# Dealing the keys of a K or V half tile by sixteenths of the head instead of by halves

## The chip, the cores and the metric

The kernel runs on one core of one Trainium2 chip. The metric is the device time of one execution in microseconds (us). Runs of one kernel agree within about 0.3% in most executions; the three runs of the kernel before gave 311.65, 312.02 and 314.75 us, with a median of 312.02 us.

## The reference: two layers of attention over a cache and a gated GLU, one token each

Four sequences (B = 4) decode one token through two layers with the same weights and the same cache. Each layer adds grouped-query attention and then a gated linear unit to the residual x.

```python
def _A_ref(x, k_cache, v_cache, wq, wo):          # x: [4, 1, 512]
    q = (x @ wq).reshape(B, Sq, Hq, Dh)...        # Hq = 32 heads of Dh = 128
    k = jnp.repeat(k_cache, rep, axis=1)          # k_cache: [4, 8, 4096, 128] bf16, rep = 4
    v = jnp.repeat(v_cache, rep, axis=1)
    scores = jnp.einsum("bhqd,bhkd->bhqk", q, k) * (Dh ** -0.5)
    p = _softmax(scores, axis=-1)
    o = jnp.einsum("bhqk,bhkd->bhqd", p, v)
    return o... @ wo

def _B_ref(x, w_gate, w_up, w_down):              # F = 1792
    h = _sigmoid(x @ w_gate) * (x @ w_up)
    return h @ w_down

x = x + _A_ref(_layernorm(x), ...)
x = x + _B_ref(_layernorm(x), ...)
x = x + _A_ref(_layernorm(x), ...)                # the same cache and weights again
x = x + _B_ref(_layernorm(x), ...)
```

A head of the cache has 4096 keys of 128 bf16 numbers, 256 bytes a key and 1 MB a head. Softmax and the sum over the keys don't depend on the order of the keys, as long as K and V are put in the same order.

## The kernel before: units, half tiles and a ring of 23 slots

**Units.** The attention is cut into 16 units (b, hg, l): sequence, group of four cache heads (NS = 4 heads s of the group), layer. `UNITS` gives their order. The heads of hg = 1 stay in SBUF between the layers, so a unit (b, 1, 1) loads nothing; every other unit loads its four heads of K and of V. `unit_scores`, `unit_probs` and `unit_values` write the work of a unit.

**Half tiles.** A head of K or V is loaded in two half tiles q = 0 and 1 of 2048 keys: `load_kv` (lines 508 to 516) issues one DMA of 512 KB from the queue of SyncE (SP) at line 514. Its destination is a slot of `ring`, 128 partitions by `TH * DH` = 2048 bf16 numbers, so 4 KB in each partition: 16 keys. Its source (line 513) is a run of 512 KB of the head, the front half of the head for q = 0 and the back half for q = 1. Partition p gets keys 16p to 16p + 15 of that half.

**Loads.** There are 192 such DMAs (96 of K and 96 of V), 100.7 MB of the 114.6 MB that the kernel reads. The rest are the weights: `wq` in two loads (line 519, 2 MB each), `wo` in four of 1 MB, and `wg`, `wu`, `wd` of 1.75 MB each. `LOADS` fixes the order of all loads by hand; a word such as K0000 stands for two half tiles (two heads s of one q). K comes with q outermost, V with the pair of heads outermost.

**Order of the work.** `_Plan.schedule` places every operation in a simulated time with costs written beside it (a K or V load has `size=0.524, cost=0.5`), chooses a ring slot for each load (the slot that comes free first of 23), and adds matmuls into a scratch bank (line 1105) where TensorE would idle. `emit` then writes the instructions of each engine with waits on semaphores. A load waits on SP for the last user of its slot.

**Use.** A K half tile is transposed in place by VectorE (line 723, 32 by 32 blocks of pairs of bf16), four matmuls of each half tile read it into the scores (line 731), VectorE takes the maximum (754 to 761), ScalarE the exponential (line 768), and the probabilities are transposed and spread (774, 779, 789). The values matmuls (line 815) read V slots as they lie. Nothing in these lines names a key by its place in the head: the key in partition p, place t of slot q of K meets the key in the same place of V.

Of the kernel before, what the change touches and what calls it, by code (L numbers as in the profile page):

```python
# [350 lines left out]
def bass_interleave_layers__gqa_block_cached__glu_gated_glu__decode_kernel(nc, A_x, A_k, A_v, A_wq, A_wo, B_x, B_wg, B_wu, B_wd, out):  # L351
# [5 lines left out]
    P = 128  # L357
# [4 lines left out]
    NS = 4  # L362
# [4 lines left out]
    TH = T // 2  # L367
# [127 lines left out]
    def tile(kind, b, hg, l, s, q):  # L495
        if l == 1 and hg == 1 and (s, q) in kept[kind]:
            l = 0
        key = (kind, b, hg, l, s, q)
        if key not in tiles:
            tiles[key] = _Tile(key)  # L500
        return tiles[key]

    def fresh(kind, hg, l, s, q):
        return not (l == 1 and hg == 1 and (s, q) in kept[kind])
# [3 lines left out]
    def load_kv(kind, u, s, q):  # L508
        b, hg, l = u
        if not fresh(kind, hg, l, s, q):  # L510
            return
        t = tile(kind, b, hg, l, s, q)
        src = (A_k if kind == "k" else A_v)[b, hg * NS + s, q * TH * P:(q + 1) * TH * P].rearrange("(p t) d -> p (t d)", p=P)
        S.put("sp", lambda e: e.dma_start(ring[t.slot], src), dma="ring", load=t, size=0.524, cost=0.5)  # L514
        sent[0] += 0.524 / DMA_RATE
        place[kind, u, s, q] = sent[0]
# [33 lines left out]
    for word in LOADS.split():  # L550
        if word[:2] == "wq":
            load_wq(int(word[2]))
        elif word[:2] == "wo":
            load_wo(int(word[2]))
        elif word[0] == "w":
            load_glu(word)
        else:
            for piece in pieces(word[0], word[1:]):
                load_kv(*piece)
# [586 lines left out]
```

## Time and profile before

| what | value |
|---|---|
| median of 3 runs | 312.02 us (311.65 to 314.75) |
| the profiled execution | 312.2 us, span 310.5 us |
| bytes read from HBM | 114.56 MB, 369 GB/s over the span |
| packets of SP's queue (q1) | 34832, 94.6% of 16 DMA engines' span |
| VectorE (DVE) busy | 168.1 us (54%) |
| TensorE (PE) busy | 213.2 us (69%), 50.5 us of it fillers of line 1105 |
| ScalarE (ACT) busy | 60.8 us (20%) |
| K and V loads, issue to landing | medians 9.7 and 10.2 us |

The span is the time from the first to the last instruction of the profiled execution; 1.7 us of that execution lie outside it. The page cuts the span into 40 slices of 7.8 us; the row GB/s has what the DMA engines moved in each. A packet is what one of the 16 DMA engines moves as one piece; SP's queue has 128 packets of 4 KB for a half tile and 16 packets of 4 bytes that raise the semaphore.

### The profile page before, as it was taken

The numbers are of one execution on the slowest core, as the hardware profiler recorded it, in microseconds if no ns is written. First come the engines' busy times: TensorE is split into PE (matmuls) and PEld (weight loads), VectorE is DVE, ScalarE is ACT, GpSimd is POOL, SyncE is SP. The second block draws the span as 40 slices with busy tenths as digits, with TensorE's granted clock in tenths as the row PEclk, the third lists the DMA queues.
The fourth block names the chain that finished last, engine by engine and source line by source line (L and its number), as shares of the span: only waits on it lengthen the run. The fifth ranks groups of instructions, "written<-read, shape, count | busy, mean of one in ns | idle before, by whom it ended". The sixth has DMA issues, their size and how long they took to land.

```text
span 310.5 us, 7729 instructions
## 1 busy us (share of the span) xinstructions
PE 213.2 (69%) x3395; PEld 114.2 (37%) x3395; DVE 168.1 (54%) x314; ACT 60.8 (20%) x151; POOL 12.6 (4%) x44
## 2 busy tenths in 40 slices
PE   1344446577838976776996866885974757788694
PEld 1213114433425632243553422462431424534243
DVE  3675542483001699596217863736996952475112
ACT  0202002002101312021323120131330213231301
POOL 8000000000000000000000000000000000000001
PEclk9999999959995998599978877997897999979859
DMA  7999999999999999999999999799999999999900
GB/s 265 411 408 410 409 388 348 395 410 409 404 397 411 402 409 407 407 411 395 380 413 385 409 410 406 283 340 408 331 414 410 408 401 373 394 352 411 391 9 4
DMA packets 34931, 115.09 MB, mean 371 GB/s; under 512 B 3280, under 2 KB 7376, under 8 KB 34896
## 3 DMA queue, kind: packets, MB, share of 16 engines
q1 hardware_dynamic: 34832, 114.57, 94.6%
q8 instruction: 27, 0.44, 0.6%
q14 instruction: 8, 0.07, 0.1%
q10 hardware_dynamic: 64, 0.01, 0.0%
HBM read 114.56 MB, written 0.00 MB: 369 GB/s over the span
## 4 chain that ended last, share of the span: by engine, by line
DMA 57%; PE 25%; DVE 8%; SPq 4%; issue 3%; ACT 3%; POOL 1%; DVEq 0%; ACTq 0%
DMA ring<-in_A_k_cache_dram 20%; DMA ring<-in_A_v_cache_dram 17%; DMA wd<-in_B_w_down_dram 7%; PE S_ps L731 7%; DMA wq<-in_A_wq_dram 6%; DMA wo<-in_A_wo_dram 5%; PE O_ps L815 5%; DVE ring L723 4%; SPq L514 3%; PE M_ps L850 2%; PE Q_ps L651 2%; PE G_ps L954 1%; PE PT_ps L1105 1%; SPq L519 1%; PE PT_ps L779 1%
## 5 line engine op out<-in xcount | busy, mean ns | idle before, releaser
L723 DVE STREAM_TRANSPOSE ring<-ring 128x1024 int32<-128x1024 int32 x96 | 116.1, 1227 | 33.4 <-DMA ring<-in_A_k_cache_dram 32.6
L731 PE MATMUL S_ps<-ring,qz 128*32 128x512 bf16 x512 | 48.4, 505 | 32.7 <-DVE ring L723 26.0
L815 PE MATMUL O_ps<-ring,pt_sb 128*16 128x512 bf16 x512 | 45.4, 442 | 20.5 <-DMA ring<-in_A_v_cache_dram 17.5
L1105 PE MATMUL PT_ps<-even 128*128 128x256 bf16 x305 | 50.5, 305 | 8.9 <-ACT pp L932 4.3
L1105 PEld LDWEIGHTS PT_ps<-even 128*128 128x128 bf16 x305 | 29.1, 109 | 27.5 <-issue 9.8
L827 ACT ACTIVATE b<-O_ps 128x512 bf16<-128x512 f32 x32 | 19.1, 596 | 85.3 <-PE O_ps L815 81.8
L731 PEld LDWEIGHTS S_ps<-ring,qz 128*32 128x32 bf16 x512 | 13.9, 113 | 55.5 <-DVE ring L723 31.5
L768 ACT ACTIVATE pp<-S_ps,tr 128x512 bf16<-128x512 f32 x16 | 13.2, 828 | 50.4 <-DVE tr L761 48.5
L754 DVE TENSOR_REDUCE stat<-S_ps 128x1 f32<-128x512 f32 x16 | 11.1, 692 | 21.9 <-PE S_ps L731 21.8
L815 PEld LDWEIGHTS O_ps<-ring,pt_sb 128*16 128x16 bf16 x512 | 9.7, 89 | 32.8 <-issue 13.1
L850 PE MATMUL M_ps<-oT,wo 128*128 128x32 bf16 x512 | 15.8, 178 | 2.0 <-DMA wo<-in_A_wo_dram 1.6
L839 DVE TENSOR_TENSOR oT<-M_ps,rl 128x8 bf16<-128x8 f32 x32 | 4.9, 152 | 22.7 <-PE M_ps L832 22.7
L850 PEld LDWEIGHTS M_ps<-oT,wo 128*128 128x128 bf16 x512 | 14.1, 97 | 7.3 <-DVE oT L839 2.9
L902 POOL TENSOR_TENSOR stat<-stat 128x1 f32<-128x1 f32 x8 | 4.4, 545 | 256.2 <-ACT stat L898 256.2
L789 ACT ACTIVATE pt_sb<-PT_ps 128x512 bf16<-128x512 f32 x16 | 9.6, 597 | 17.6 <-PE PT_ps L779 17.6
L832 PE MATMUL M_ps<-sel_o,b 128*128 128x32 bf16 x128 | 8.7, 183 | 4.7 <-ACT b L827 4.6
L832 PEld LDWEIGHTS M_ps<-sel_o,b 128*128 128x128 bf16 x128 | 5.8, 101 | 16.1 <-ACT b L827 12.3
L937 DVE SCALAR_TENSOR_TENSOR b<-pp,U_ps 128x448 bf16<-128x448 f32 (+2 forms) x6 | 3.2, 538 | 14.5 <-ACT pp L932 12.9
L695 ACT ACTIVATE maskrs<-mask,stat 128x16 f32<-128x16 f32 x16 | 4.5, 304 | 28.5 <-DVE qz L700 26.5
L793 PE MATMUL M_ps<-sel_h,stat 128*128 128x16 f32 x32 | 6.7, 286 | 4.4 <-ACT pp L768 4.1
L774 DVE STREAM_TRANSPOSE pp<-pp 128x256 int32<-128x256 int32 x16 | 6.8, 426 | 5.2 <-ACT pp L768 5.2
L700 DVE TENSOR_TENSOR qz<-Q_ps,maskrs 128x256 bf16<-128x256 f32 x16 | 6.3, 394 | 6.0 <-PE Q_ps L690 6.0
(112 smaller groups left out, 162.6 us busy)
## 6 DMA issues: line engine op xcount, KB each, us to landing
ring<-in_A_k_cache_dram SPq DMA_DIRECT2D x96, 512.0 KB, 9.7
ring<-in_A_v_cache_dram SPq DMA_DIRECT2D x96, 512.0 KB, 10.2
wq<-in_A_wq_dram SPq DMA_DIRECT2D x2, 2048.0 KB, 13.8
wo<-in_A_wo_dram SPq DMA_DIRECT2D x4, 1024.0 KB, 14.7
wg<-in_B_w_gate_dram SPq DMA_DIRECT2D x1, 1792.0 KB, 16.1
wu<-in_B_w_up_dram SPq DMA_DIRECT2D x1, 1792.0 KB, 20.2
wd<-in_B_w_down_dram SPq DMA_DIRECT2D x1, 1792.0 KB, 22.7
xin<-in_A_x_dram ACTq DMA_DIRECT2D x1, 4.0 KB, 3.4
```

The costliest lines, as they stand in the source:

```text
L514: S.put("sp", lambda e: e.dma_start(ring[t.slot], src), dma="ring", load=t, size=0.524, cost=0.5)
L723: "dve", lambda e, t=t: e.transpose(ring[t.slot].bitcast(dt.int32), ring[t.slot].bitcast(dt.int32)),
L731: fns.append(lambda e, s=s, t=t, nn=nn, q=q: e.matmul(S_ps[qi][32 * s:32 * s + 32, :], lhsT=window(qi, s * NQ + nn, q), rhs=ring[t.slot].r ...
L754: dve(lambda e: e.tensor_reduce(ml[at], bank, AX.X, ALU.max, negate=True), keys(f"S{qi}", ss), keys("ml", ss), 0.7)
L768: lambda e: e.activation(p_sb[at].rearrange("p (t j r) -> p t r j", j=32, r=2), bank.rearrange("p (t r j) -> p t r j", r=2, j=32), ACTF.Ex ...
L774: dve(lambda e: e.transpose(pd[at].bitcast(dt.int32), p_sb[at].bitcast(dt.int32)), [own("P")], [own("P") + "d"], 0.4)
L789: "act", lambda e: e.activation(pt_sb[qi][:, cols], PT_ps[:, cols], ACTF.Copy),
L815: fns.append(lambda e, m=m, at=at, v=v, c=c, q=q: e.matmul(O_ps[m:m + 16, :], lhsT=pt[:, at:at + 16], rhs=ring[v.slot][:, c * 512:(c + 1) ...
L827: "act", lambda e: e.activation(b1[:], O_ps[:], ACTF.Copy),
L832: fns.append(lambda e, tt=tt: e.matmul(M_ps[:, 0:WIDE], lhsT=b1[:, tt * P:(tt + 1) * P], rhs=sel_o[:, tt, :].unsqueeze(1).broadcast_to([P, ...
L850: fns.append(lambda e, k=k, n=n, h0=h0: e.matmul(M_ps[:, k * WIDE:(k + 1) * WIDE], lhsT=wo[:, h0 + n, k * P:(k + 1) * P], rhs=oT[:, b, h0 ...
L1105: S.filler(lambda e: e.matmul(PT_ps[:, 0:256], lhsT=ident, rhs=flat_even[:, 0:256], start=True, stop=True), "PT")
```

## The change: the half of each sixteenth

```diff
@@ load_kv
         t = tile(kind, b, hg, l, s, q)
-        src = (A_k if kind == "k" else A_v)[b, hg * NS + s, q * TH * P:(q + 1) * TH * P].rearrange("(p t) d -> p (t d)", p=P)
+
+        src = (A_k if kind == "k" else A_v)[b, hg * NS + s].rearrange("(e h j t) d -> h e j (t d)", e=16, h=2, j=8)[q]
         S.put("sp", lambda e: e.dma_start(ring[t.slot], src), dma="ring", load=t, size=0.524, cost=0.5)
```

The head is cut into 16 stretches e of 256 keys (64 KB). Each stretch has a front half and a back half h of 128 keys (32 KB), and each half has 8 groups j of t = 16 keys (4 KB). Half tile q takes half h = q of every stretch, so its source is now a pattern of 16 by 8 by 2048 numbers: 16 pieces of 32 KB whose starts lie 64 KB apart. Partition 8e + j gets group j of piece e. K and V change alike. Sizes, the order of the loads, the ring, the plan's costs and every other instruction stay.

## The prediction

> **What bounds the kernel now.** I read the page first, from its slices and queues to the chain, then the windows, then the ring's own view, then SP's waits. The page:
>
> ```profile
> span 310.5 us, 7729 instructions
> ...
> DMA  7999999999999999999999999799999999999900
> GB/s 265 411 408 410 409 388 348 395 410 409 404 397 411 402 409 407 407 411 395 380 413 385 409 410 406 283 340 408 331 414 410 408 401 373 394 352 411 391 9 4
> ...
> q1 hardware_dynamic: 34832, 114.57, 94.6%
> ...
> DMA 57%; PE 25%; DVE 8%; SPq 4%; issue 3%; ACT 3%; POOL 1%; DVEq 0%; ACTq 0%
> ```
>
> The DMA engines are busy in nearly every slice until the loads end, and slice after slice stands at 407 to 411 GB/s. The chain that ended last is 57% DMA. So the stream of loads bounds the kernel, and the rate of that stream is what any change of a load is worth. The windows (columns: stretch, its length, busy time of PE, PEld, DVE, ACT and POOL with instruction counts, granted clock, DMA share, GB/s) show what sets the rate:
>
> ```profile
> 13.00:25.00 12.00, 4.01 (x36) 1.09 (x36) 8.81 (x12) 1.41 (x4) 0.00 (x0) 1.00 1.02 408
> 48.00:52.00 4.00, 2.39 (x59) 2.00 (x58) 1.03 (x4) 1.35 (x3) 0.00 (x0) 1.00 1.10 348
> 112.00:128.00 16.00, 10.25 (x125) 4.92 (x121) 15.46 (x20) 3.05 (x7) 0.00 (x0) 0.79 1.03 409
> 187.00:197.00 10.00, 7.92 (x118) 4.13 (x119) 5.06 (x9) 0.60 (x1) 0.00 (x0) 0.83 1.03 408
> 197.00:206.00 9.00, 6.71 (x122) 3.37 (x120) 4.84 (x12) 3.33 (x9) 0.54 (x1) 1.00 0.73 259
> 206.00:220.00 14.00, 10.65 (x214) 6.06 (x209) 8.18 (x17) 2.21 (x9) 0.55 (x1) 0.77 0.95 370
> 270.00:283.00 13.00, 11.21 (x157) 4.38 (x157) 8.76 (x16) 4.24 (x11) 0.00 (x0) 0.87 0.95 364
> 283.00:296.00 13.00, 9.91 (x188) 5.49 (x188) 3.81 (x13) 2.71 (x6) 0.00 (x0) 0.84 0.93 371
> ```
>
> With K and V in flight (112 to 128, 187 to 197) the engines are full (share 1.03) and move 409 GB/s. A packet of 4096 bytes then takes 16 x 4096 / 409 GB/s = 160 ns, and a half tile, 8 packets on each of 16 engines, 1.28 us. At 48 to 52 us `wo` comes in packets of 1 KB and the rate is 348 GB/s, 47.1 ns a packet. So 3 KB more cost 113.1 ns, 37.7 ns a KB, and 9.4 ns of each packet don't depend on its size. The last four rows have the engines partly idle or slow: against 409 GB/s they lose 9 x (1 - 259/409) = 3.3, then 1.3, 1.4 and 1.2 us, in all 7 us.
>
> ```profile
> L514 SPq DMA_DIRECT2D ring<-in_A_k_cache_dram x96: 327/433/4366, 1.3 to 275.0; - x96
> L514 SPq DMA_DIRECT2D ring<-in_A_v_cache_dram x96: 327/433/12672, 12.3 to 282.1; - x96
> ...
> DMA to landing us min/median/max: 3.7/10.0/23.4
> ```
>
> SP needs 433 ns (median) for an issue, a third of the 1.28 us that the load then takes, and a load lands 10.0 us after its issue: about eight half tiles stand in the queue. SP's own waits are for slots:
>
> ```profile
> SPq L514 <- PE O_ps L815: 26.0, 12, 9.0
> ...
> SPq L514 <- PE S_ps L731: 10.5, 8, 4.6
> ```
>
> These waits are for readers of old tiles and mostly lie under the eight tiles still queued.
>
> **The change part by part.** Removed and added instructions: none. There are still 192 DMAs of 512 KB on the same queue in the same order; the plan sees the same `size` and `cost`, so every engine's program and the slots stay. Keys move between the halves in K and V alike, so the sums see the same pairs.
>
> *Addresses in HBM.* A tile's source is 16 pieces of 32 KB with gaps of 32 KB instead of one run. `wq` is the nearest row: its packets are 4 KB rows 8 KB apart, so eight neighbouring partitions start 64 KB from the next eight. It is in flight up to 25 us, mixed with K and V, at 408 GB/s, the rate of K and V alone. Price 0. Bound: 408 against 409 is 0.25% of 192 x 1.28 = 246 us, 0.6 us.
>
> *SP.* The issue has a source of three dimensions now. `wq` had three too, and its first issue takes 0.41 us in the timeline of SP. Price 0, hidden under the eight queued tiles. If an issue took twice 433 ns it would still be under 1.28 us; only where the queue has run dry (around 197 us, and at the head) would 0.43 us show, three or four times: up to 2 us.
>
> *Which engine writes which partition.* This is the open part. [...] Now the source counts 16 first, and each of those stretches fills partitions 8e to 8e + 7. An engine that takes one stretch writes eight neighbouring partitions, and must. The trace doesn't show which partitions an engine wrote before, nor what two engines cost each other when they write through one way into SBUF. The lower bound is nothing: a packet stays at 160 ns, and 1.28 us a tile. The upper bound is that, in step, two engines always share what one had: 320 ns a packet, 2.56 us a tile, 246 us more. [...] If the two run in step, but data in flight lets one packet of each four escape, the factor is 1.75; if they run exactly out of step it is 1.0. I take the middle, 1.375, because nothing in the plan puts the engines in or out of step. Cost 0.375 x 246 = 92 us.
>
> [...]
>
> *What a slower stream gives back.* The 7 us in which the stream lagged behind readers or slots go, since compute then has more time for each tile. DVE's 168 us and PE's 213 us hide under the loads. The weights (13.9 MB) and the tail of 14 us after the last landing stay.
>
> **Sum.** 310.5 + 92 - 7 = 395.5 us of span, and 1.7 us outside it: 397 us. The profiled execution's 312.2 us stand 0.2 us over the median of the runs, so no shift is needed. With the bounds of the factor alone the case reaches from 312 to 551 us; what I count as this case is a factor of 1.15 to 1.85, 342 to 514 us.
>
> **Rivals.**
>
> *Nothing happens: 312 us.* The queue may deal the rows as before, or the meetings may be hidden by data in flight, or the change doesn't do what it says at the engines. For it: `wq` shows that addresses alone cost nothing, and SP and the plan don't change. Against it: the engines have no slack (share 1.03), so any extra wait of a packet shows in full.
>
> *The reads become longer: faster, 305 us.* The 32 KB of an engine are one straight piece, and could be read as one packet instead of eight. Seven of eight fixed costs of 9.4 ns go, 8.2 ns of 160 for each 4 KB: 5.1% of 246 us, 12.6 us. Only 57% of the chain is DMA, so some 7 us arrive: 305 us; all of it would be 299. For it: the 348 and 409 GB/s of the two packet sizes. Against it: the pattern still names 8 groups of 2048 numbers, and before, where the whole 512 KB was straight, packets were 4 KB.
>
> *The meetings stay rare: 324 us.* Engines that start in step part quickly, each meeting pushing one behind the other until they alternate. Then only the beginnings pay: a factor of 1.05 is 12 us. For it: the stretches that lose rate make the engines start anew only a few times. It ends slower, like the forecast, but its profile would show about 390 GB/s.
>
> **How the numbers follow.** Forecast (partners meet) 0.50; rare meetings 0.14; nothing 0.16; longer reads 0.20. A difference of under 1% can't be told from no change here. Of "nothing", 0.13 lies within 1%, and of the rest half falls on each side; of "longer reads", 0.01 falls within 1%. Faster 0.015 + 0.19, about 0.21; same 0.14; slower 0.50 + 0.14 + 0.015, about 0.65. The range leaves out 0.1 below, where longer reads arrive nearly in full, and 0.1 above, where partners run nearly in step: 302 to 490 us. It is wide because one unknown factor between 1 and 2 stands on 246 us of a stream that bounds the kernel.
>
> **What the profile after would show.** Instructions stay at 7729. If I am right, the slices of K and V stand well under 409 GB/s with the DMA share still near 1, at about 300 GB/s; the slices with `wo`, `wg`, `wu` and `wd` alone keep 348 to 400; a load lands later than 10.0 us after issue; VectorE's waits for K (32.6 us) and the values' waits for V (17.5 us) grow; the chain is more than 57% DMA; SP's waits for slots shrink. If packets of q1 fall from 34832 to some 13000, the reads became longer. If GB/s stays at 409 with the same packets, partners don't meet, and I was wrong in the term of the dealing. A lower rate in the slices of the weights alone would mean that something other than the dealing slowed the engines.

## The result: 447.7 us against 312.0 us, and the profile after

The median of four runs is 447.74 us (442.38 to 453.05), that of before 312.0 us. The ratio is 1.419, with a 95% interval of 1.405 to 1.432. It is taken over undisturbed runs alone, so it is a little smaller than the quotient of the two medians. The profiled execution took 445.58 us, with a span of 443.9 us.

From the page of the profile after: the span, the DMA share and GB/s of the 40 slices (now 11.1 us each), SP's queue, and the engines' shares of the chain.

```profile
span 443.9 us, 7729 instructions
...
DMA  8999999999999999999999999899999999999950
GB/s 260 241 307 247 247 245 346 251 259 260 376 287 255 254 256 261 259 261 270 284 298 285 296 296 299 244 239 244 252 262 266 266 277 265 259 255 249 248 140 3
...
q1 hardware_dynamic: 34832, 114.57, 98.0%
...
DMA 67%; PE 14%; SPq 12%; DVE 4%; issue 2%; ACT 1%; POOL 0%; DVEq 0%
```

The same 34832 packets keep the engines busier than before (98.0% of the span, up from 94.6%), and move 239 to 299 GB/s where K and V are loaded, down from 410. Only slices with much weight traffic stand out, at 307, 346 and 376 GB/s. The packets' own time shows where the difference went:

- Time that packets of SP's queue took, per engine: 0.946 x 310.5 = 293.7 us before, 0.980 x 443.9 = 435.0 us after, 141.3 us more.
- The span grew by 443.9 - 310.5 = 133.4 us. The sum of packet times is not the time in which the engines are busy: packets of a full engine overlap, and a window with full engines stands at a share of 1.03. So the rest of the span, 16.8 us before and 8.9 us after, is not idle time; the stretch after the last landing alone is 14.0 us before and 14.3 us after.

If all of the 141.3 us belongs to the 246 us of K and V, a packet of 4 KB takes 1.57 times as long, 252 ns. The windows after agree (columns as in the prediction; the first two have weights in flight, the third K and V, the last nothing):

```profile
73.00:78.00 5.00, 3.98 (x51) 3.21 (x52) 0.16 (x1) 0.00 (x0) 0.00 (x0) 1.00 1.13 352
117.00:122.00 5.00, 4.13 (x39) 2.59 (x37) 0.41 (x3) 0.73 (x4) 0.55 (x1) 0.90 1.03 400
290.00:405.00 115.00, 72.02 (x1013) 35.79 (x1013) 50.70 (x88) 19.18 (x51) 1.62 (x3) 0.67 1.03 258
429.60:443.90 14.30, 10.12 (x154) 5.34 (x154) 3.23 (x17) 1.82 (x5) 1.01 (x1) 0.74 0.01 3
```

`wo` keeps its rate (352 GB/s, 348 before), and so do the weights of the GLU (400 GB/s; 399 at 80 to 92 us before). Their lines of the program did not change. Only K and V are slower, at 258 GB/s or 16 x 4096 / 258 = 254 ns a packet.

From the ring's own view of the profile after (each line: operation, count, duration in ns as min/median/max), and from the waits:

```profile
L515 SPq DMA_DIRECT2D ring<-in_A_k_cache_dram x96: 536/599/6136, 1.3 to 394.1; - x96
L515 SPq DMA_DIRECT2D ring<-in_A_v_cache_dram x96: 536/598/17772, 15.4 to 405.1; - x96
...
DMA to landing us min/median/max: 5.0/16.4/30.2
```

```profile
DVE ring L724 <- DMA ring<-in_A_k_cache_dram: 112.5, 78, 8.1
PE O_ps L816 <- DMA ring<-in_A_v_cache_dram: 82.3, 33, 11.4
```

An issue on SP takes 599 ns instead of 433, a load lands 16.4 us after its issue instead of 10.0, and VectorE's waits for K and the values' waits for V have grown from 32.6 and 17.5 us to these. Nothing else on the engines explains 133 us: VectorE is busy for 172.3 us, 4 more than before. TensorE is busy for 246.4 us instead of 213.2, at a granted clock of 0.741 instead of 0.899, but its share of the chain fell from 25% to 14%. Why the clock fell is not shown. SP's share of the chain rose from 4% to 12%. Most of that lies in the first 47 us, where many of its issues last 1.8 to 2.1 us while the engines are full (share 1.03). This fits an SP that is held up by a full queue; no run separates it.

### The profile page after: what moved, and what is told of

It reads as the page before. It is cut to its first block, busy times and chain, and to the rows that moved or that the text cites. A ratio compares the mean times of both kernels' runs of the same rounds, so it can differ in the third digit from the quotient of the medians.

```text
span 443.9 us, 7729 instructions
## 1 busy us (share of the span) xinstructions
PE 246.4 (56%) x3395; PEld 124.4 (28%) x3395; DVE 172.3 (39%) x314; ACT 60.5 (14%) x151; POOL 12.5 (3%) x44
## 3 DMA queue, kind: packets, MB, share of 16 engines
q1 hardware_dynamic: 34832, 114.57, 98.0%
## 4 chain that ended last, share of the span: by engine, by line
DMA 67%; PE 14%; SPq 12%; DVE 4%; issue 2%; ACT 1%; POOL 0%; DVEq 0%
DMA ring<-in_A_v_cache_dram 31%; DMA ring<-in_A_k_cache_dram 29%; SPq L515 11%; DMA wo<-in_A_wo_dram 6%; PE O_ps L816 4%; PE S_ps L732 4%; DVE ring L724 2%; PE PT_ps L1106 1%; PE G_ps L913 1%; PE M_ps L851 1%; PE U_ps L913 1%; SPq L520 1%; PE G_ps L955 1%; DVE stat L755 0%; PE M_ps L833 0%
## 5 line engine op out<-in xcount | busy, mean ns | idle before, releaser
L724 DVE STREAM_TRANSPOSE ring<-ring 128x1024 int32<-128x1024 int32 x96 | 118.7, 1239 | 112.8 <-DMA ring<-in_A_k_cache_dram 112.5
L816 PE MATMUL O_ps<-ring,pt_sb 128*16 128x512 bf16 x512 | 55.0, 521 | 86.0 <-DMA ring<-in_A_v_cache_dram 82.3
L732 PE MATMUL S_ps<-ring,qz 128*32 128x512 bf16 x512 | 51.9, 534 | 61.3 <-DVE ring L724 49.0
L1106 PE MATMUL PT_ps<-even 128*128 128x256 bf16 x305 | 60.3, 347 | 9.8 <-ACT pp L933 5.3
L1106 PEld LDWEIGHTS PT_ps<-even 128*128 128x128 bf16 x305 | 32.2, 119 | 33.2 <-issue 11.6
L828 ACT ACTIVATE b<-O_ps 128x512 bf16<-128x512 f32 x32 | 19.1, 597 | 143.5 <-PE O_ps L816 141.3
L851 PE MATMUL M_ps<-oT,wo 128*128 128x32 bf16 x512 | 16.7, 185 | 3.9 <-DVE oT L840 2.2
L780 PE MATMUL PT_ps<-pp,even 128*32 128x128 bf16 x256 | 9.2, 288 | 3.0 <-DVE oT L840 2.0
L794 PE MATMUL M_ps<-sel_h,stat 128*128 128x16 f32 x32 | 8.5, 346 | 2.3 <-ACT pp L769 2.0
```

Of the source, the lines that this page charges most:

```text
L724: "dve", lambda e, t=t: e.transpose(ring[t.slot].bitcast(dt.int32), ring[t.slot].bitcast(dt.int32)),
L732: fns.append(lambda e, s=s, t=t, nn=nn, q=q: e.matmul(S_ps[qi][32 * s:32 * s + 32, :], lhsT=window(qi, s * NQ + nn, q), rhs=ring[t.slot].r ...
L780: fns.append(lambda e, s=s, a=a: e.matmul(PT_ps[32 * a:32 * a + 32, s * P:(s + 1) * P], lhsT=ident[at, 32 * s:32 * s + 32], rhs=spread[:, ...
L816: fns.append(lambda e, m=m, at=at, v=v, c=c, q=q: e.matmul(O_ps[m:m + 16, :], lhsT=pt[:, at:at + 16], rhs=ring[v.slot][:, c * 512:(c + 1) ...
L828: "act", lambda e: e.activation(b1[:], O_ps[:], ACTF.Copy),
L851: fns.append(lambda e, k=k, n=n, h0=h0: e.matmul(M_ps[:, k * WIDE:(k + 1) * WIDE], lhsT=wo[:, h0 + n, k * P:(k + 1) * P], rhs=oT[:, b, h0 ...
```

## The experiments

Theory 1 is that of the forecast: the dealing of eight neighbouring partitions to one engine makes engines meet on the way into SBUF. Theory 2 blames the gaps between the pieces in HBM. Theory 3 blames the source of three dimensions, which takes longer to issue or to expand, wherever its rows land. In what follows, "dealt by 128" and "dealt by 16" say what the source counts first.

### Addresses alone (e1)

```diff
-        src = ...[b, hg * NS + s, q * TH * P:(q + 1) * TH * P].rearrange("(p t) d -> p (t d)", p=P)
+        src = ...[b, hg * NS + s].rearrange("(p h t) d -> h p (t d)", p=P, h=2)[q]
```

> Addresses alone: a half tile is the front or back 4 KB of each 8 KB of the head, so it is spread over the whole 1 MB as in the change, but source and destination both count 128 rows. Theory 1 (the dealing of eight neighbouring partitions to one engine makes engines meet on the SBUF side): about 312 us, 409 GB/s in the slices of K and V, 160 ns a packet. Theory 2 (the gaps between the pieces in HBM slow the reads): well over 400 us, slices near 260 GB/s.

328.37 us against 314.59 us of before on the same chip: ratio 1.045 (1.040 to 1.050). Both theories missed the size. Spreading a half tile over 1 MB in pieces of 4 KB does cost something, 14 us, but a tenth of what the change cost. From the page, the slices:

```profile
GB/s 272 390 410 390 354 393 350 399 412 407 401 401 374 352 412 410 408 335 347 383 353 340 407 411 409 277 354 389 329 410 388 367 366 372 300 282 366 401 48 4
```

Some stretches run at 407 to 412 GB/s like before, others at 277 to 393; before has about half as many slices below 395. Theory 2 can't be the main cause. What slows these stretches is taken up in e5.

### Dealing alone (e2)

```diff
-        src = ...[b, hg * NS + s, q * TH * P:(q + 1) * TH * P].rearrange("(p t) d -> p (t d)", p=P)
+        src = ...[b, hg * NS + s, q * TH * P:(q + 1) * TH * P].rearrange("(j e t) d -> e j (t d)", e=16, j=8)
```

> [...] Theory 1: 440 to 455 us, slices of K and V near 255 GB/s. Theory 2: about 312 us. Theory 3 (a source of three dimensions is slower to issue or to expand into descriptors, wherever the rows land): 440 to 455 us as well; the next kernel tells 1 from 3.

The median is 456.06 us (446.15 to 467.16). The profiled execution took 452.26 us with a span of 450.5 us, against 445.58 and 443.9 us for the change. The tile is the same run of 512 KB as before, counted 16 first (4 KB apart) and then 8 (64 KB apart), and all of the loss is there. From its page:

```profile
GB/s 265 249 307 249 250 256 330 248 248 249 393 262 254 255 260 262 262 270 280 278 286 299 304 316 315 195 232 232 233 235 236 235 241 241 244 252 258 268 165 3
...
q1 hardware_dynamic: 34832, 114.57, 98.0%
```

The slices have the form of the change's own, at the same share of 98.0%. Theory 2 has fallen as the main cause; theories 1 and 3 stand.

### Loads alone, and where the rows land (e3)

```python
...
# stage e; stage f is the same with partitions (0, 64)
for i in range(36):
    load(e, slot(i, (32, 96)), heads[i].rearrange("(e h j t) d -> h e j (t d)", e=16, h=4, j=4)[0])
...
```

> Loads alone: all of the computation is left out and zeros are written. Stages follow each other, each of 24 half tiles of 512 KB without a wait between them: a the source of before, b that of the change, c the spread one dealt by 128, d the run dealt by 16; then 36 loads of 256 KB with a source of 16 pieces of 16 KB, e into partitions 32 to 95 and f into partitions 0 to 63; then a and b again. Theory 1: a and c near 409 GB/s, b and d 220 to 300. [...] Theory 2: a, d near 409, b, c, e, f slower. Theory 3: a, c near 409, b, d, e, f slower, and e as f.

Windows inside the stages a, b, c, d, e and f, in this order (stretch, its length, busy time of POOL, granted clock, DMA share, GB/s):

```profile
8.00:28.00 20.00, 0.00 (x0) 1.00 1.02 411
38.00:84.00 46.00, 0.00 (x0) 1.00 1.03 246
94.00:112.00 18.00, 0.00 (x0) 1.00 1.03 412
125.00:172.00 47.00, 0.00 (x0) 1.00 1.03 237
188.00:200.00 12.00, 0.00 (x0) 1.00 1.03 411
210.00:250.00 40.00, 0.00 (x0) 1.00 1.03 200
```

Stages e and f have the same sources, the same dimensions, the same number of issues on SP and the same packets. Only the partitions differ: 32 to 95 run at 411 GB/s, 0 to 63 at 200. That ends theory 3: a source of three dimensions runs at 411 GB/s, the rate of stage a, in partitions 32 to 95. Shown is that the place of the rows in SBUF alone can halve the rate of the same loads, from 411 to 200 GB/s. Stages b and d fill all 128 partitions and still stand at 246 and 237 GB/s, where c has spread addresses and runs at 412. With the addresses and the dimensions out, what is left for b and d is which partitions are written together. That two engines meet there is argued from this and from e4; no run shows it.

Stages e and f write into 64 partitions, so they give the price of a place and not that of the change's own tiles, which fill 128. Which engine fills which partitions is not in the trace. That one engine gets eight neighbouring partitions of a tile is the author's assumption, and theory 1 rests on it.

### One load at a time, and the length of the rows (e4)

```python
...
one_by_one(8, slot, run), one_by_one(8, slot, sixteenths),                  # each waits for the one before
together(40, short, run_short), together(40, short, sixteenths_short),      # rows of 2 KB
together(24, slot, run), together(24, slot, sixteenths),                    # rows of 4 KB
together(16, long, run_long), together(16, long, sixteenths_long),          # rows of 8 KB
...
```

> Loads alone again, computation left out and zeros written. First 8 half tiles that each wait for the one before to land, with the source of before, then with that of the change: under theory 1 all engines start in step, every packet meets its partner, and a tile takes up to 1.28 us more from issue to landing; if data in flight hides meetings, much less. Then pairs of stages, dealt by 128 and dealt by 16, with rows of 2 KB, 4 KB and 8 KB a partition. By the fixed 9.4 ns a packet, dealt by 128: 386, 409 and 421 GB/s. Dealt by 16: if engines stay in step whatever the length, all three near half of that; if data in flight hides a fixed amount of each meeting, the short rows lose least and the long ones most; under theory 3 the short rows lose most.

One at a time, from the DMA issues in a window of each stage (KB each, median us from issue to landing), with the source of before and then that of the change:

```profile
ring<-in_A_k_cache_dram SPq DMA_DIRECT2D x8, 512.0 KB, 3.3
...
ring<-in_A_k_cache_dram SPq DMA_DIRECT2D x6, 512.0 KB, 4.8
```

A load takes 1.5 us more, but not all of this passes while its packets move. The trace's records of single packets divide it (medians of each stage). The first packet starts 1.33 us after the start of the issue instead of 0.96; the issue itself takes 537 ns instead of 328. From there the 128 packets need 2.8 us instead of 2.0 to the last one's end, and the landing follows 0.66 us later instead of 0.34. So while the packets move, the load loses about 0.8 us, less than the 1.28 us of the upper bound. The expectation had all engines start in step and every packet meet its partner. The records show neither: the sixteenth packet of a load starts 0.2 to 0.8 us after its first, and 37 to 48 of the 128 packets take under 165 ns (93 to 109 when dealt by 128).

The windows of the three pairs, each dealt by 128 and then by 16, for rows of 2, 4 and 8 KB:

```profile
70.00:90.00 20.00, 0.00 (x0) 1.00 1.05 388
100.00:130.00 30.00, 0.00 (x0) 1.00 1.05 276
140.00:165.00 25.00, 0.00 (x0) 1.00 1.03 411
172.00:222.00 50.00, 0.00 (x0) 1.00 1.03 240
230.00:258.00 28.00, 0.00 (x0) 1.00 1.02 425
270.00:340.00 70.00, 0.00 (x0) 1.00 1.01 217
```

Dealt by 128, the rates of 388, 411 and 425 are near the 386, 409 and 421 expected from a fixed 9.4 ns a packet. Dealt by 16, packets take 1.41, 1.71 and 1.96 times as long: longer rows lose more. That is against theory 3, by which short rows lose most. None of the three passes 2, the upper bound of the prediction. With rows of 2 KB a packet takes 118.7 - 84.5 = 34 ns more, where the bound is 84.5 ns; with 4 KB it is 114 of 159 ns, with 8 KB 296 of 308 ns. So packets of 2 and 4 KB stay 50 and 46 ns under the doubled time, those of 8 KB 13 ns. The expectation's fixed amount does not hold. The three sources dealt by 16 are not quite alike: the rows of 8 KB come from one run, like d in e3, the others from separate pieces, like b, and b and d differ by 4%. What holds the shorter rows under the doubled time was not shown.

### The spread reads in the kernel's order (e5)

```python
spread = lambda A, b, g, q: A[b, g].rearrange("(p h t) d -> h p (t d)", p=P, h=2)[q]
phases = [together(k_order(), run), together(k_order(), spread), together(v_order(), run),
          together(v_order(), spread), together(in_turn(), run), together(in_turn(), spread)]
```

> Loads alone (computation left out, zeros written), all dealt by 128: what made e1 4.5% slower when its pattern ran at 404 to 410 GB/s by itself in e3? Six stages of 24 half tiles: K in the kernel's order (halves outermost) as runs, then spread; V in the kernel's order (pairs of heads outermost) as runs, then spread; K and V in turn, four words each as in the list of loads, as runs, then spread. If the order of the heads and halves or the mix of K and V makes the spread reads slow, its stage stands some 5 to 15% under 409 GB/s and the runs do not. If all six stand at 409, the loss in e1 comes only beside the computation.

```profile
6.00:30.00 24.00, 0.00 (x0) 1.00 1.02 411
40.00:64.00 24.00, 0.00 (x0) 1.00 1.02 405
76.00:98.00 22.00, 0.00 (x0) 1.00 1.03 409
108.00:132.00 24.00, 0.00 (x0) 1.00 1.02 396
145.00:168.00 23.00, 0.00 (x0) 1.00 1.02 408
180.00:204.00 24.00, 0.00 (x0) 1.00 1.01 388
```

Runs: 411, 409 and 408 GB/s. Spread: 405 for K alone, 396 for V alone, 388 for K and V in turn. So addresses matter a little once both halves of a head, and K with V, are read close together: 1.5% for K alone, 3% for V alone and 5% in the mix, with no computation beside it. 5% of the 246 us of K and V are 12 us, near the 14 us of e1. Why such reads slow each other stays open.

### The fixed cost of a packet, in the kernel (e6)

e4 pointed to longer rows, dealt by 128, as a way to beat the kernel before.

```diff
...
-    SLOTS = 23
+    SLOTS = 11
-    ring = [sb(f"ring{i}", [P, TH * DH], bf)[:] ...]
+    ring = [sb(f"ring{i}", [P, T * DH], bf)[:] ...]
-        src = ...[b, hg * NS + s, q * TH * P:(q + 1) * TH * P].rearrange("(p t) d -> p (t d)", p=P)
+        src = ...[b, hg * NS + s].rearrange("(p t) d -> p (t d)", p=P)
...
```

The list of loads, the transposes and the matmuls are fitted to whole heads, so the plan of the other engines changes too.

> The fixed cost of a packet in the kernel itself: a head of K or V is loaded whole, 32 keys and 8 KB a partition, dealt by 128, into 11 slots of 1 MB instead of 23 of 0.5 MB. e4 gave 411 GB/s for rows of 4 KB and 425 for rows of 8 KB, so the 100.7 MB of K and V take about 8 us less if the stream stays full: 304 to 306 us against 312. With coarser slots, one half slot fewer and K and V arriving in larger steps the stream may run dry more often: then 312 to 325 us, with more slices under 400 GB/s.

355.52 us against 314.2 us: ratio 1.129 (1.118 to 1.139). From its page:

```profile
GB/s 287 421 412 423 409 348 404 422 355 400 418 265 420 421 352 384 125 428 258 283 421 423 420 126 2 294 416 427 416 357 361 117 301 275 279 283 427 417 53 3
```

The packets do gain: full slices reach 420 to 428 GB/s. But the stream stops again and again (125, 126, 2, 117). In the longest of these gaps SP waits 36.9 us for the matmuls that read an old K tile (`SPq L343 <- PE S_ps L731`), and its waits of this kind grew from 61.1 to 131.8 us. So slots come free too late; how much of this is the coarse ring and how much the new plan was not separated. The loss is five times the 8 us at stake, and more than the 325 us that I allowed for. No version here beats the kernel before.

## Why the prediction was right, and what it mis-sized

The forecast was that partners meet, 397 us, with 342 to 514 us for the case itself. 447.7 us lies in it. The step that the forecast rests on, a cause on the SBUF side, held: e2 has the loss with the old run of bytes, and in e3 the place of the rows in SBUF alone moves the rate between 411 and 200 GB/s. That pairs of engines share one way in is supported by e4, where the factor rises to 1.96 with long rows and does not pass 2; it was not seen directly. The whole range of 302 to 490 us held any factor from 1 to 1.75, so landing in it says little about the size, and the 397 us came from a middle without a measurement behind it.

- **The dealing, 92 us.** This is the term that was too small. The span grew by 133.4 us. If nothing came back, the dealing cost 133 us, and if the 7 us below came back in full, about 140: a factor of 1.54 to 1.57 where I took 1.375. I had halved the way from 1.75 to 1, as if engines were as likely to run out of step as in step. No run shows the 1.75 or the 1.375. In their place the runs showed 1.54 to 1.57 in the kernel, first packets that start 0.2 to 0.8 us apart rather than in step (e4), and 1.71 in a stream without computation (411 against 240 GB/s, e4). Why the kernel stands lower, with slices between 239 and 299 GB/s, was not settled.
- **The give-back, 7 us.** Not measured by itself, since the packets' share counts overlaps. Part of it did not come: from 405 to 429.6 us, before the last landing, the engines are still partly idle (share 0.94, 231 GB/s), a loss of 24.6 x (1 - 231/258) = 2.6 us.
- **Addresses, 0.** `wq` at 408 GB/s was too narrow a basis for a general zero: e1 shows 14 us for the finest spread. For the change's own pieces of 32 KB, e2 with the old run of bytes is no faster (span 450.5 against 443.9 us), so no part of the loss shows as theirs.
- **SP, 0.** The issue grew to 599 ns, inside the bound of twice 433. `wq` was not the right row for it: its first issue takes 0.43 us after the change as well. The growth stayed covered: stage e of e3 issues a load of 256 KB every 0.64 us and still moves 411 GB/s.
- **The rivals.** Nothing happens: fell with the second slice (241 GB/s, 411 before). Longer reads: fell with 34832 packets, none of them wider. Rare meetings: its 390 GB/s is nowhere in the stretches of K and V.
- **The signs foretold.** Instructions, packets, landing times, the waits for K and V, and the chain's share of DMA (57% to 67%) came as said, and so did the rate of the weights (352 and 400 GB/s); the slices lie lower than the 300 GB/s named. One was wrong: SP's waits for slots did not shrink. The prediction's lines had left out the largest of them, the waits at line 343, where `emit` writes a wait of its own: 61.1 us in 11 waits for readers of K. These and the waits for readers of V (26.0 us in 12 before) are now:

```profile
SPq L343 <- PE S_ps L732: 86.0, 11, 12.1
...
SPq L515 <- PE O_ps L816: 28.0, 9, 11.4
```

The readers themselves wait longer for their tiles (the waits for K and V above), which fits slots that come free later.

## What to carry to other kernels

When a load's source and destination count different outermost dimensions, its rate can fall by 40% with the same bytes (411 to 237 GB/s, stages a and d of e3), much more than the orders of bytes in HBM tried here cost (5% at most, 408 to 388 GB/s, e5): keep 128 rows outermost on both sides where the stream bounds the kernel. That the source decides which partitions one DMA engine fills is the author's reading; no trace shows it. To tell an SBUF cause from an HBM or an issue cause, load the same source into other partitions and compare GB/s (411 and 200 in stages e and f of e3). A gain of some per cent a packet from longer rows (425 against 411 GB/s, e4) did not pay here (355.52 against 314.2 us, e6), where the ring lost its fine slots for it.

## What was not expected of the hardware

- An issue on SP takes 599 ns (median) with the source that counts 16 first, 433 ns with 128 rows (loads one at a time: 537 and 328 ns, e4).
- The first sixteen packets of a load do not start together: dealt by 16, the sixteenth starts 0.2 to 0.8 us after the first, dealt by 128 0.2 to 0.5 us (e4).
- The loss in the dealing by 16 grows with the row: 1.41, 1.71 and 1.96 times the packet time for 2, 4 and 8 KB (e4).
- Pieces of 4 KB, 8 KB apart, read at 412 GB/s when only front halves of heads are read (e3, stage c), and at 388 GB/s when both halves of K and V heads are mixed (e5).
